# Windowed attention with a squared-ReLU feed-forward on one core: the attention probabilities of nine chunks are transposed by DVE in 32 by 32 blocks

## The chip, the cores and the metric

The kernel runs on one core of one Trainium2 chip. Its time is the device time of one launch in microseconds (us); the median of several runs counts. A core has these engines, each with its own in-order queue: PE (TensorE, matmuls; its weight loads are shown apart as PEld), DVE (VectorE), ACT (ScalarE), POOL (GpSimd) and SP (SyncE, which here issues all DMAs). They wait for each other through semaphores. PSUM is the memory that PE writes; SBUF holds everything else.

## The reference, cut to what matters

```python
B, H, S, D = 4, 8, 768, 64        # batch, heads, positions, head width
block, window = 32, 16            # nb = S // block = 24 blocks
k_sum = k.reshape(B, H, nb, block, D).max(axis=3)
v_sum = v.reshape(B, H, nb, block, D).mean(axis=3)
scores_l = scale * q @ k.T        # kept only where |i - j| < window
scores_s = scale * q @ k_sum.T + log(block)
a = softmax(concatenate([scores_l, scores_s]))
attn = a @ concatenate([v, v_sum])
x = attn.transpose(0, 2, 1, 3).reshape(B * S, H * D)      # 3072 x 512
r = maximum(x @ w_in, 0)                                  # 512 -> 2048
out = (s * r * r + b) @ w_out                             # 2048 -> 512
```

## The kernel before

The 3072 rows are worked off in 12 chunks `c` of T = 256 rows, three to a batch. A chunk has eight heads as four pairs `p`; a pair's two heads `e` lie in the two halves of the 128 partitions. A chunk's rows are four subtiles of 64; each sees a window of 96 keys and the 24 block maxima, so KR = 120 columns.

The attention of one pair goes through these helpers. `scores` (L280) multiplies queries by the 120 keys into PSUM (`ps`). `masked` (L306) lets DVE add the mask and take the extreme of each row, `exps` (L328) is the exponential on ACT, and `normalize` (L336) multiplies by the reciprocal of the sum on DVE. The result `pr` holds 128 rows (two subtiles) in each of four parts of 120 columns. The values matmul needs the 120 columns on the partitions, so `transposes` (L344) turns each part on PE into PSUM (`pt`), and `turned` (L355) copies 120 by 512 from there to SBUF (`pT`) on ACT. `values` (L371) multiplies `pT` by `vw`, the 96 windowed rows of v and below them the 24 block means; a pair takes 16 matmuls of PE, 64 for a chunk. `attended` and `attended_low` make the high and low parts (`xh`, `xl`) of the result on ACT and DVE.

The block means of a batch are made once, in the step before its first chunk's values: `v_sum` (L168) sums blocks on DVE (`vhalf`, six instructions), `v_mean` (L174) scales on ACT (`vmean`) and sends the rows by SP's DMAs to `vsum`, and `fill_v` (L260) copies them into `vw` on POOL. The sums free the buffers for the last loads of v (`load_v`), which stand in SP's queue ahead of the loads of `vw` and `qk` and of the DMAs to `vsum`. `fill_k` copies the maxima into the keys on POOL.

The feed-forward treats the 2048 hidden columns as 16 steps `f` of 128, and two of them as a double block `q` (q0 to q7). `hidden` makes `ph` in PSUM (L434, three matmuls for each of four parts, as high and low parts are multiplied apart), four steps to a hidden block. `activate` is ReLU and square on ACT (L442, L448), `scaled` is s and b on POOL (L455), and `upper_rows` and `lower_rows` make `gh` and `gl` on DVE (L219, L466). `project` (L478) multiplies them by w_out into `po`.

While PE does the feed-forward of chunk c-1, the attention of chunk c is made beside it. The order on all engines is written out: every call is put down with a step (16 to a chunk, `base` is the step before the chunk's first) and a kind, and calls are issued by step and then by kind. For chunks up to c = 2 and the first hidden steps a list by hand (`FIRST_ORDER`) is used. In a chunk's cycle PE does a hidden block (12 x 4 matmuls), a projection (24), and so on, four times; at step `base + 16` stand the values of chunk c and the scores of chunk c+1. The transposes of pairs 0 and 1 stand at step `base + 8`, those of pairs 2 and 3 at `base + 12`, each behind a hidden block.

Of the kernel before, what the change touches and what calls it, by code (L numbers as in the profile page):

```python
# [11 lines left out]
F32 = mybir.dt.float32  # L12
# [7 lines left out]
P = 128  # L20
B, H, S, D = 4, 8, 768, 64
DM, DFF = 512, 2048
BLOCK = 32
WINDOW = 16
SUB = 64
WIN = SUB + 2 * WINDOW
NB = S // BLOCK
KR = WIN + NB
NSUB = 4
T = NSUB * SUB  # L30
# [14 lines left out]
def windowed_attention_then_relu2_ffn(ctx, tc, qk, vwin, kt, vt, kq, vrow, wp, out):  # L45


    nc = tc.nc
# [5 lines left out]
    p2 = ctx.enter_context(tc.tile_pool(name="p2", bufs=2))  # L54
# [29 lines left out]
    def mask_of(st):  # L84
        return mask_first if st == 0 else mask_last if st == NST - 2 else mask_mid
# [3 lines left out]
    def at(step, order, fn, *args):  # L89
        plan[step].append((order, len(plan[step]), fn, args))  # L90
# [5 lines left out]
    for base, sign in ((0, 1), (BLOCK - 1, -1)):  # L96
        nc.gpsimd.affine_select(
            out=mean4[:, NB - 4 : NB], in_=mean4[:, NB - 4 : NB], compare_op=ALU.is_ge, fill=0.0,
            base=base, pattern=[[-sign * BLOCK, 4]], channel_multiplier=sign,
# [117 lines left out]
    def copy(by_dve, out_, in_):  # L217
        if by_dve:
            nc.vector.tensor_copy(out_, in_)  # L219
        else:  # L220
            nc.scalar.copy(out_, in_)  # L221
# [7 lines left out]
    def place(c):  # L229
        return c // PER_B, c % PER_B  # L230

    sb_of = {}
    qk_t, vw_t, ps_of, pr_of, mn_of, sm_of, pt_of, pT_of, o_of, xt, xl = ({} for _ in range(11))
# [42 lines left out]
    def together(c):  # L276

        return c >= 2
# [27 lines left out]
    def masked(c, p, j):  # L306
        _, ci = place(c)
        if j == 0 and c == 0:
            t = stage.tile([P, 4 * KR + 8], F32, name="pr0", tag="stage")
            pr_of[c, p] = t[:, : 4 * KR].rearrange("p (n k) -> p n k", k=KR)  # L310
            mn_of[c, p], sm_of[c, p] = t[:, 4 * KR : 4 * KR + 4], t[:, 4 * KR + 4 :]
        elif j == 0:
            t = p2.tile([P, 4 * KR + 16], F32, name="pr", bufs=4)
            pr_of[c, p] = t[:, : 4 * KR].rearrange("p (n k) -> p n k", k=KR)
            mn_of[c, p] = p2.tile([P, 4], F32, name="mn", bufs=4)
            sm_of[c, p] = p2.tile([P, 4], F32, name="sums", bufs=4)
        for e in range(2):
            n = 2 * e + j
            nc.vector.tensor_tensor_reduce(  # L319
                out=pr_of[c, p][:, n, :], in0=ps_of[c, p][e][:, j, :], in1=mask_of(NSUB * ci + 2 * j),  # L320
                scale=-1.0 / math.sqrt(D), scalar=3.0e38, op0=ALU.add, op1=ALU.min,
                accum_out=mn_of[c, p][:, n : n + 1],
            )
        if j == 1:
            ps_of.pop((c, p))
            qk_t.pop((c, p))
# [9 lines left out]
    def normalize(c, p, other=False):  # L336
# [4 lines left out]
        pr = pr_of[c, p]  # L341
        nc.vector.tensor_tensor(pr, pr, rs.unsqueeze(2).to_broadcast([P, 4, KR]), ALU.mult)  # L342

    def transposes(c, p):  # L344
        pr = pr_of.pop((c, p))
        if c == 2:
            pt_of[c, p] = ps_s.tile([P, 4 * P], F32, name="pt", tag="ps")
        elif together(c) and p % 2:
            pt_of[c, p] = ps_v.tile([P, 4 * P], F32, name="pt", tag="pav")
        else:  # L350
            pt_of[c, p] = ps_t.tile([P, 4 * P], F32, name="pt")
        for n in range(4):
            nc.tensor.transpose(pt_of[c, p][:KR, n * P : (n + 1) * P], pr[:, n, :], ident)  # L353

    def turned(c, p, other=False):  # L355
        if c == 0 and p > 1:
            pT_of[c, p] = held["vn", 1][:KR, 1024 + 512 * (p - 2) : 1024 + 512 * (p - 1)]
        else:
            pT_of[c, p] = p2.tile([KR, 4 * P], F32, name="pT", bufs=4)
        copy(other, pT_of[c, p], pt_of.pop((c, p))[:KR])  # L360

    def values_of_means(p):
        pT, o = pT_of.pop((0, p)), o_of[0, p]
        for i in range(NSUB):
            for e in range(2):
                nc.tensor.matmul(
                    o[64 * e : 64 * e + 64, i * SUB : (i + 1) * SUB], vsum[0][0:KR, 2 * p + e],
                    pT[:, e * T + i * SUB : e * T + (i + 1) * SUB], start=False, stop=(i == NSUB - 1),
                )

    def values(c, p):  # L371
        vw, pT = vw_t.pop((c, p)), pT_of[c, p] if c == 0 else pT_of.pop((c, p))
        if c == 0 and p % 2:
            o_of[c, p] = ps_po.tile([P, DM], F32, name="pav", tag="po")
        elif c < 2 or p % 2 == 0:
            if c == 2:
                o_of[c, p] = ps_s.tile([P, 2 * T], F32, name="pav", tag="ps")
            elif together(c) and p:
                o_of[c, p] = ps_t.tile([P, 2 * T], F32, name="pav", tag="pt")
            else:  # L380
                o_of[c, p] = ps_v.tile([P, 2 * T], F32, name="pav")
            if c > 1:
                o_of[c, p + 1] = o_of[c, p][:, T:]
        o = o_of[c, p]
        for i in range(NSUB):
            for e in range(2):
                oi, pi = o[64 * e : 64 * e + 64, i * SUB : (i + 1) * SUB], pT[:, e * T + i * SUB : e * T + (i + 1) * SUB]
                if c == 0:
                    nc.tensor.matmul(oi, vw[0:WIN, e, i, :], pi[0:WIN], start=(i == 0), stop=False)
                else:  # L390
                    nc.tensor.matmul(oi, vw[:KR, e, i, :], pi, start=True, stop=True)  # L391

    def attended_part(c, p):
        kcs = slice(p, p + (1 if c < 2 else 2))
# [93 lines left out]
        nc.sync.dma_start(out[r0 : r0 + P, :], o)  # L488


    LOAD, SPLIT, ATT, NEXT, WEIGHTS, HID, PE_ATT, CHAIN, VISIT, PROJ, EVICT = range(11)


    FIRST = -100
# [25 lines left out]
    def of(fn, *more):  # L520
# [4 lines left out]
        "i": of(load_weights, "in"), "o": of(load_weights, "out"), "w": of(load_weights, "in", "out"),  # L525
        "u": load_unit, "x": load_values, "L": load_k,
        "W": keep_warm, "K": k_max, "k": fill_k, "Z": scores_of_maxima, "S": scores, "M": masked, "E": exps,
        "N": normalize, "T": transposes, "C": turned, "V": values, "U": values_of_means, "R": mean_of_rows,
        "F": mean_done, "t": fill_v, "X": attended, "y": attended_low, 
        "Ai": of(scale_weights, "in"), "Ao": of(scale_weights, "out"), "A": of(scale_weights, "both"),  # L530
# [20 lines left out]
    def then(step, order, fn, *args):  # L551
        if (fn, args) not in ahead:
            at(step, order, fn, *args)

    for c in range(2, NC):
        bi, ci = place(c)
        for p in range(NPAIR):
            base, v_at = NF * (c - 1) - 1, (9, 10, 4, 5)[p]
            tr = 8 + 4 * (p // 2)
            lags = (1, 1, 1, 2, (12, 13, 11, 11)[p], tr, tr, 16, 17)  # L560
            m, e0, e1, n, fv, tr, tu, va, xa = (base + lag for lag in lags)
            if ci == 0:
                then(base - 12 + p, LOAD, load_k, bi, p)
                then(base - 7 + p, ATT, k_max, bi, p)
                if p < 2:
                    for third in range(3):
                        then(base + v_at - 5 + third, LOAD, load_v, bi, p, third)
                        then(base + v_at - 1 + third // 2, ATT, v_sum, bi, p, third)
                    then(base + v_at + 1, ATT, v_mean, bi, p)
            then(base - 6, LOAD, load_unit, c, p)  # L570
            then(base + v_at, LOAD, load_values, c, p)
            then(base - 2, ATT, fill_k, c, p)
            for j in range(2):
                then(base, VISIT, scores, c, p, j)
                then(m, NEXT if p < 2 else ATT, masked, c, p, j)
                then((e0, e1)[j], NEXT if p < 2 else ATT, exps, c, p, j)
            then(n, ATT, normalize, c, p)
            then(fv, ATT, fill_v, c, p)
            then(tr, PE_ATT, transposes, c, p)
            then(tu, CHAIN, turned, c, p)  # L580
            then(va, VISIT, values, c, p)
            if p % 2 == 0:
                then(xa, ATT, attended, c, p)
                then(xa, ATT, attended_low, c, p)
# [3 lines left out]
    for i in range(NF, NC * NF):  # L588
        c, f = divmod(i, NF)
# [69 lines left out]
```

## Time and profile before

| | |
|---|---|
| median of 3 runs | 624.66 us (624.11 to 624.74) |
| the profiled execution | 624.84 us |
| its span, first to last instruction | 622.7 us |
| distance between two chunks' values on PE (from 313.77 to 363.41 us) | 49.64 us |

The profile describes one execution. Its page gives the busy time of each engine, the granted TensorE clock in 40 slices, the chain of work that ended last, and groups of like instructions with count, busy time and mean duration. A timeline lists single instructions: start in us, length in us, engine, line, output and inputs, and in brackets how long the engine had been idle and what released it. The length includes the filling and emptying of an engine's pipeline, so on PE and DVE an instruction may start before the one ahead has ended; the distance of starts tells the rate.

### The profile page before, as it was taken

Reading aid. Unit: us, or ns where it says so; the run is one execution under the profiler, and the core shown is the slowest. Engines: PE = TensorE matmul, PEld = TensorE weight load, DVE = VectorE, ACT = ScalarE, POOL = GpSimd, SP = SyncE. Lnnn points to the kernel's source line nnn. Section 1 sums busy time; section 2 is a strip of 40 time slices with the busy share of each in tenths; the row PEclk is TensorE's granted clock in tenths of the full one; section 3 lists DMA queues with packets and bytes.
Section 4 is the critical chain, followed back from the end, with each engine's and each line's share of the span. In section 5 each row is a group of like instructions: output and inputs, shape, how many; then the busy total and the mean of one; then the engine's idle time right before and its main releaser. Section 6 shows DMA issues by size and latency. Waiting matters only on the chain.

```text
span 622.7 us, 13558 instructions
## 1 busy us (share of the span) xinstructions
PE 612.3 (98%) x5384; PEld 553.7 (89%) x5384; DVE 292.2 (47%) x838; ACT 294.2 (47%) x748; POOL 135.5 (22%) x257
## 2 busy tenths in 40 slices
PE   6999999999999999999999999999999999999997
PEld 5788999899999989998999899999998998899896
DVE  6999988755441262363262243444426126212211
ACT  5999997353353352363264253334335336222221
POOL 4320013111411410411311401321141041131110
PEclk9999999999999999999999999999999999999999
DMA  8998722126005107005304012500700500200000
GB/s 343 379 402 343 274 79 99 46 79 214 20 15 168 31 14 275 2 18 146 124 19 150 33 45 91 187 18 35 233 20 2 182 1 19 85 2 1 35 2 34
DMA packets 26991, 66.41 MB, mean 107 GB/s; under 512 B 3824, under 2 KB 3824, under 8 KB 26928
## 3 DMA queue, kind: packets, MB, share of 16 engines
q1 hardware_dynamic: 26928, 65.54, 30.1%
q8 instruction: 42, 0.69, 0.5%
q14 instruction: 21, 0.17, 0.1%
HBM read 59.09 MB, written 6.29 MB: 105 GB/s over the span
## 4 chain that ended last, share of the span: by engine, by line
PE 93%; ACT 3%; DMA 2%; DVE 1%; issue 0%; SPq 0%; DVEq 0%; ACTq 0%
PE po L478 43%; PE ph L434 41%; PE pav L391 3%; PE pt L353 3%; PE ps L301 3%; ACT pr L332 1%; DMA wraw<-in_wp_dram 1%; DMA kq<-in_kq_dram 1%; DVE pr L342 0%; ACT wraw L122 0%; ACT wraw L123 0%; DVE ksum L156 0%; ACT vsum L221 0%; ACT r L442 0%; ACT r L453 0%
## 5 line engine op out<-in xcount | busy, mean ns | idle before, releaser
L219 DVE CAST gh<-r 128x512 fp32r<-128x512 f32 x88 | 37.7, 428 | 278.0 <-POOL r L455 269.1
L455 POOL TENSOR_SCALAR r<-r,sb_col 128x512 f32<-128x512 f32 x85 | 67.9, 799 | 408.2 <-ACT r L448 308.9
L478 PE MATMUL po<-wh,gl 128*128 128x512 f32 x384 | 153.3, 399 | 0.0
L478 PE MATMUL po<-wh,gh 128*128 128x512 f32 x384 | 151.2, 394 | 0.0
L478 PE MATMUL po<-wl,gh 128*128 128x512 f32 x384 | 150.2, 391 | 0.0
L442 ACT ACTIVATE r<-ph 128x512 f32<-128x512 f32 x93 | 55.8, 600 | 191.4 <-PE ph L434 178.7
L434 PE MATMUL ph<-xh,wl 128*128 128x256 f32 x760 | 118.8, 279 | 0.2 <-ACT r L442 0.2
L434 PE MATMUL ph<-xl,wh 128*128 128x256 f32 x760 | 117.5, 277 | 0.0
L434 PE MATMUL ph<-xh,wh 128*128 128x256 f32 x760 | 117.4, 277 | 0.0
L434 PEld LDWEIGHTS ph<-xh,wl 128*128 128x128 f32 x760 | 104.6, 188 | 5.6 <-ACT r L442 0.7
L434 PEld LDWEIGHTS ph<-xl,wh 128*128 128x128 f32 x760 | 101.0, 188 | 0.0
L434 PEld LDWEIGHTS ph<-xh,wh 128*128 128x128 f32 x760 | 100.4, 188 | 0.0
L478 PEld LDWEIGHTS po<-wh,gh 128*128 128x128 f32 x384 | 72.2, 188 | 15.5
L478 PEld LDWEIGHTS po<-wh,gl 128*128 128x128 f32 x384 | 72.2, 188 | 14.8 <-issue 1.4
L478 PEld LDWEIGHTS po<-wl,gh 128*128 128x128 f32 x384 | 72.2, 188 | 14.0
L332 ACT ACTIVATE pr<-pr,mn 128x120 f32<-128x120 f32 x176 | 66.9, 382 | 19.4 <-DVE mn L319 19.3
L466 DVE TENSOR_TENSOR gl<-r,gh 128x512 fp32r<-128x512 f32 x96 | 67.9, 708 | 4.1 <-ACT gh L221 1.3
L448 ACT ACTIVATE r<-r 128x512 f32<-128x512 f32 x92 | 58.2, 632 | 5.7 <-DVE r L444 2.9
L263 POOL COPY vw<-vsum 24x256 f32<-24x256 f32 x88 | 47.3, 572 | 29.6 <-DMA vsum<-vmean 10.2
L221 ACT COPY pT<-pt 120x512 f32<-120x512 f32 x44 | 23.9, 585 | 30.0 <-PE pt L353 29.8
L221 ACT COPY o<-po 128x512 f32<-128x512 f32 x23 | 13.5, 585 | 46.1 <-PE po L478 45.0
L342 DVE TENSOR_TENSOR pr<-pr,rs 128x480 f32<-128x480 f32 x48 | 32.1, 669 | 2.4 <-ACT pr L332 0.5
(86 smaller groups left out, 505.2 us busy)
## 6 DMA issues: line engine op xcount, KB each, us to landing
wraw<-in_wp_dram SPq DMA_DIRECT2D x32, 512.0 KB
qk<-in_qk_dram SPq DMA_DIRECT2D x44, 369.0 KB
vw<-in_vwin_dram SPq DMA_DIRECT2D x48, 256.0 KB
out_dram<-o SPq DMA_DIRECT2D x24, 256.0 KB
kraw<-in_kt_dram SPq DMA_DIRECT2D x12, 384.0 KB
vraw<-in_vt_dram SPq DMA_DIRECT2D x12, 252.0 KB
kq<-in_kq_dram SPq DMA_DIRECT2D x4, 512.0 KB
vraw<-in_vt_dram SPq DMA_DIRECT2D x6, 264.0 KB
```

Of the source, the lines that this page charges most:

```text
L219: nc.vector.tensor_copy(out_, in_)
L221: nc.scalar.copy(out_, in_)
L263: nc.gpsimd.tensor_copy(vw_t[c, p][WIN:KR, e], vsum[bi][WIN : WIN + NB, 2 * p + e, :].unsqueeze(1).to_broadcast([NB, NSUB, D]),)
L301: nc.tensor.matmul(o, qi, kw[r, i, :], start=True, stop=True)
L332: nc.scalar.activation(pr, pr, AF.Exp, bias=mn_of[c, p][:, n : n + 1], scale=-1.0, accum_out=sm_of[c, p][:, n : n + 1])
L342: nc.vector.tensor_tensor(pr, pr, rs.unsqueeze(2).to_broadcast([P, 4, KR]), ALU.mult)
L434: nc.tensor.matmul(ph, w[:, kc * P : (kc + 1) * P], x[:, kc], start=(n == 0), stop=(n == len(terms) - 1))
L442: nc.scalar.activation(r, ph, AF.Relu)
L448: nc.scalar.activation(r, r, AF.Square)
L455: (nc.vector if other else nc.gpsimd).tensor_scalar(g, g, s_col, b_col, ALU.mult, ALU.add)
L466: nc.vector.tensor_tensor(gl, g, gh.bitcast(F32), ALU.subtract)
L478: nc.tensor.matmul(po[c, t], a[:, t * P : (t + 1) * P], w[:, 512:], start=(f == 0 and n == 0), stop=(f == NF - 1 and n == len(terms) - 1),)
```

## The change

For chunks c > 2 the eight transposes on PE and the copy by ACT go. In their place `turned_blocks` issues, for each pair and each group `a` of 32 rows, four `nc.vector.transpose`: each takes 32 partitions and 32 columns of all four parts, turns the four 32 by 32 blocks, and writes them to the partitions 32k to 32k + 31 of `pT`. 120 columns are not a multiple of 32, so the fourth takes columns 96 to 127 through a view shifted by 8; eight columns behind the last part are set to zero by POOL (`memset`), and rows 120 to 127 of `pT` are not read. A new kind of call, TURN, stands behind CHAIN and ahead of VISIT; the sixteen calls of a chunk are spread over the steps `base + 3` to `base + 15`. `pT` has 128 partitions in place of 120.

```diff
             pr_of[c, p] = t[:, : 4 * KR].rearrange("p (n k) -> p n k", k=KR)
+            if turns_on_dve(c):
+                nc.gpsimd.memset(t[:, 4 * KR : 4 * KR + 8], 0.0)
+                wide_of[c, p] = t[:, 8 : 4 * KR + 8].rearrange("p (n k) -> p n k", k=KR)
...
+    def turns_on_dve(c):
+        return c > 2
+
+    def turned_blocks(c, p, a):
+
+        if a == 0:
+            pT_of[c, p] = p2.tile([P, 4 * P], F32, name="pT", bufs=4)
+        to = pT_of[c, p].rearrange("p (n q) -> p n q", q=P)
+        rows = slice(BLOCK * a, BLOCK * (a + 1))
+        for k in range(4):
+            src = (pr_of[c, p][rows, :, BLOCK * k : BLOCK * (k + 1)] if k < 3 else wide_of[c, p][rows, :, KR - BLOCK :])
+            nc.vector.transpose(to[BLOCK * k : BLOCK * (k + 1), :, rows], src)
...
-            pT_of[c, p] = p2.tile([KR, 4 * P], F32, name="pT", bufs=4)
-        copy(other, pT_of[c, p], pt_of.pop((c, p))[:KR])
+            pT_of[c, p] = p2.tile([P, 4 * P], F32, name="pT", bufs=4)
+        copy(other, pT_of[c, p][:KR], pt_of.pop((c, p))[:KR])
...
-                    nc.tensor.matmul(oi, vw[:KR, e, i, :], pi, start=True, stop=True)
+                    nc.tensor.matmul(oi, vw[:KR, e, i, :], pi[:KR], start=True, stop=True)
...
-    LOAD, SPLIT, ATT, NEXT, WEIGHTS, HID, PE_ATT, CHAIN, VISIT, PROJ, EVICT = range(11)
+    LOAD, SPLIT, ATT, NEXT, WEIGHTS, HID, PE_ATT, CHAIN, TURN, VISIT, PROJ, EVICT = range(12)
...
-            then(tr, PE_ATT, transposes, c, p)
-            then(tu, CHAIN, turned, c, p)
+            if turns_on_dve(c):
+                for a in range(4):
+                    then(base + 3 + (4 * p + a) * 13 // 16, TURN, turned_blocks, c, p, a)
+            else:
+                then(tr, PE_ATT, transposes, c, p)
+                then(tu, CHAIN, turned, c, p)
```

Where this moves instructions is seen at three places. The first is PE, between a hidden block and the projection behind it, in the middle of a chunk (c = 7). A row is the line, the operation, output and inputs, and the shape; "x4" are four alike. Before:

```order
L434 MATMUL ph<-xh,wl 128x256 x4
L434 MATMUL ph<-xl,wh 128x256 x4
L434 MATMUL ph<-xh,wh 128x256 x4
L353 MATMUL pt<-ident,pr 120x128 x8
L478 MATMUL po<-wh,gl 128x512
L478 MATMUL po<-wl,gh 128x512
L478 MATMUL po<-wh,gh 128x512
```

Now:

```order
L455 MATMUL ph<-xh,wl 128x256 x4
L455 MATMUL ph<-xl,wh 128x256 x4
L455 MATMUL ph<-xh,wh 128x256 x4
L499 MATMUL po<-wh,gl 128x512
L499 MATMUL po<-wl,gh 128x512
L499 MATMUL po<-wh,gh 128x512
```

The eight transposes of two pairs are gone from PE, and nothing stands in their place.

The second place is DVE in a chunk that begins a batch (c = 9), from `gh` and `gl` of q2 on, through the sums of v, to `gh` of q4. Before:

```order
L219 CAST gh<-r 128x512
L466 TENSOR_TENSOR gl<-r,gh 128x512
L172 TENSOR_REDUCE vhalf<-vraw 96x22
L172 TENSOR_REDUCE vhalf<-vraw 96x21
L219 CAST gh<-r 128x512
L466 TENSOR_TENSOR gl<-r,gh 128x512
L172 TENSOR_REDUCE vhalf<-vraw 96x21
L172 TENSOR_REDUCE vhalf<-vraw 96x22
L172 TENSOR_REDUCE vhalf<-vraw 96x21 x2
L219 CAST gh<-r 128x512
```

Now, from the twelve transposes that stand behind `gl` of q2 on:

```order
L360 STREAM_TRANSPOSE pT<-pr 32x4x32 x12
L172 TENSOR_REDUCE vhalf<-vraw 96x22
L172 TENSOR_REDUCE vhalf<-vraw 96x21
L219 CAST gh<-r 128x512
L487 TENSOR_TENSOR gl<-r,gh 128x512
L360 STREAM_TRANSPOSE pT<-pr 32x4x32 x4
L172 TENSOR_REDUCE vhalf<-vraw 96x21
L172 TENSOR_REDUCE vhalf<-vraw 96x22
L172 TENSOR_REDUCE vhalf<-vraw 96x21
L360 STREAM_TRANSPOSE pT<-pr 32x4x32 x4
L172 TENSOR_REDUCE vhalf<-vraw 96x21
L219 CAST gh<-r 128x512
```

Transposes now stand ahead of the first sum and between the sums.

The third place is DVE at the end of every chunk, from `gh` of q6 to `xl` of the finished chunk. Before:

```order
L219 CAST gh<-r 128x512
L466 TENSOR_TENSOR gl<-r,gh 128x512
L219 CAST gh<-r 128x512
L466 TENSOR_TENSOR gl<-r,gh 128x512
L407 TENSOR_TENSOR xl<-pav,xh 128x512 x2
```

Now, with the eight transposes that stand behind `gl` of q5 as the first row:

```order
L360 STREAM_TRANSPOSE pT<-pr 32x4x32 x8
L219 CAST gh<-r 128x512
L487 TENSOR_TENSOR gl<-r,gh 128x512
L360 STREAM_TRANSPOSE pT<-pr 32x4x32 x8
L219 CAST gh<-r 128x512
L487 TENSOR_TENSOR gl<-r,gh 128x512
L428 TENSOR_TENSOR xl<-pav,xh 128x512 x2
```

The last eight transposes of pair 3 stand between `gl` of q6 and `gh` of q7.

More of the change, by code (lines that the diff above doesn't have):

```diff
@@ L342, in normalize @@
         nc.vector.tensor_tensor(pr, pr, rs.unsqueeze(2).to_broadcast([P, 4, KR]), ALU.mult)
+    wide_of = {}
+    def turns_on_dve(c):
[8 more added lines that the diff above has]
+            nc.vector.transpose(to[BLOCK * k : BLOCK * (k + 1), :, rows], src)
+        if a == 3:
+            pr_of.pop((c, p))
+            wide_of.pop((c, p))
     def transposes(c, p):
@@ L367, in values_of_means @@
                     o[64 * e : 64 * e + 64, i * SUB : (i + 1) * SUB], vsum[0][0:KR, 2 * p + e],
-                    pT[:, e * T + i * SUB : e * T + (i + 1) * SUB], start=False, stop=(i == NSUB - 1),
+                    pT[:KR, e * T + i * SUB : e * T + (i + 1) * SUB], start=False, stop=(i == NSUB - 1),
                 )
```

## The prediction

> **What bounds the kernel now.** I read the busy line of the page first, then the chain that ended last, then the timeline of PE around the parts that the diff touches.
>
> ```profile
> PE 612.3 (98%) x5384; PEld 553.7 (89%) x5384; DVE 292.2 (47%) x838; ACT 294.2 (47%) x748; POOL 135.5 (22%) x257
> ...
> PE 93%; ACT 3%; DMA 2%; DVE 1%; issue 0%; SPq 0%; DVEq 0%; ACTq 0%
> PE po L478 43%; PE ph L434 41%; PE pav L391 3%; PE pt L353 3%; PE ps L301 3%; ACT pr L332 1%; DMA wraw<-in_wp_dram 1%; DMA kq<-in_kq_dram 1%; DVE pr L342 0%; ACT wraw L122 0%; ACT wraw L123 0%; DVE ksum L156 0%; ACT vsum L221 0%; ACT r L442 0%; ACT r L453 0%
> ```
>
> PE is the bound, and the transposes (pt) are 3% of its chain. Whatever leaves PE is gained, unless PE then waits for what replaces it. So there are two questions: what the transposes cost on PE, and when DVE delivers.
>
> **What leaves PE.** The timeline of PE, first where a hidden block meets a projection without transposes between, then with eight:
>
> ```profile
> 328.65 0.39 PE L478 MATMUL po<-wh,gl 128*128 128x512 f32 x1
> 328.88 0.39 PE L478 MATMUL po<-wl,gh 128*128 128x512 f32 x1
> ...
> 339.62 1.04 PE L353 MATMUL pt<-ident,pr 128*120 128x128 f32 x8
> 340.41 0.48 PE L478 MATMUL po<-wh,gl 128*128 128x512 f32 x1
> 340.73 0.40 PE L478 MATMUL po<-wl,gh 128*128 128x512 f32 x1
> ```
>
> Eight transposes hold PE from 339.62 to 340.41, 0.79 us, and the first projection matmul behind them takes 0.32 in place of 0.23: 0.88 us. Two such groups in each of nine chunks (c = 3 to 11) make 18 x 0.88 = **15.8 us** off PE, 1.76 per chunk. The copies from PSUM leave ACT too; ACT is not the bound and I count them at nothing.
>
> **What one block transpose costs.** DVE gets 16 instructions per pair, 64 per chunk, each 32 partitions by 4 x 32 columns. No row of before is one; the nearest DVE rows (groups, then two masks in the timeline, as start and length):
>
> ```profile
> L340 DVE RECIPROCAL rs<-rs 128x4 f32<-128x4 f32 x48 | 8.5, 176 | 1.3
> ...
> L342 DVE TENSOR_TENSOR pr<-pr,rs 128x480 f32<-128x480 f32 x48 | 32.1, 669 | 2.4 <-ACT pr L332 0.5
> ...
> L319 DVE DVE_READ_ACCUMULATOR2_ANT mn<- 128x1 f32 x176 | 14.7, 83 | 0.0
> ...
> 318.35 0.27 DVE L319 CUSTOM_DVE_ANT_0 pr<-ps,mask_mid 128x120 f32<-128x120 f32 x1
> ...
> 318.55 0.28 DVE L319 CUSTOM_DVE_ANT_0 pr<-ps,mask_mid 128x120 f32<-128x120 f32 x1
> ```
>
> 4 columns take 176 ns and 480 take 669: 1.04 ns a column on a base of 172. So 128 columns last about 0.30 us. Back to back, independent masks of 120 columns follow each 0.20 us, so overlap could bring 0.21; without its accumulator read of 0.08 a mask would be 0.12, the lower end. With a gap of 0.04 after each, 0.34 is the upper end. I take **0.30**, no overlap: each block writes to another partition group than the one before, which no row here does, so I do not count on the masks' overlap. [...]
>
> In total, DVE has room:
>
> ```profile
> 312.70:362.30 49.60, 49.60 (x435) 45.27 (x434) 17.40 (x62) 20.21 (x56) 11.51 (x21) 1.00 0.19 64
> ...
> 411.90:461.60 49.70, 49.70 (x435) 45.38 (x434) 21.94 (x68) 20.72 (x58) 11.03 (x21) 1.00 0.30 90
> ```
>
> The columns are PE, PEld, DVE, ACT, POOL: 64 x 0.30 = 19.2 us on top of 17.40 or 21.94 fit into the 49.6 - 1.76 = 47.8 of a chunk. But DVE is in order, and order decides.
>
> **The wait in a plain chunk.** Block transposes stand between the pairs of gh and gl that DVE makes from the hidden rows. The last eight of pair 3 stand behind gh and gl of the seventh double block (q6), and the values matmuls of pair 3 need them:
>
> ```profile
> 357.86 0.63 PE L434 MATMUL ph<-xh,wl 128*128 128x256 f32 x4
> ...
> 363.41 2.08 PE L391 MATMUL pav<-pT,vw 120*64 120x64 f32 x64
> 365.42 1.87 PE L301 MATMUL ps<-qk 64*64 64x120 f32 x64
> ...
> 360.84 0.60 ACT L442 ACTIVATE r<-ph 128x512 f32<-128x512 f32 x1 [6.50 <-PE ph L434]
> ...
> 363.01 0.43 DVE L219 CAST gh<-r 128x512 fp32r<-128x512 f32 x1 [6.47 <-POOL r L455]
> 363.47 0.69 DVE L466 TENSOR_TENSOR gl<-r,gh 128x512 fp32r<-128x512 f32 x1
> ```
>
> Count from the start of the last hidden block, 357.86. q6 is its first half; through ACT and POOL gh starts at +5.15 and gl ends at +6.30. Eight transposes bring +8.70, the signal 0.05 more. PE starts the values at +5.55 and spends 2.01 us on 64, so it stands before the third matmul of pair 3, the 51st, at +7.12. It waits 8.75 - 7.12 = **1.63 us**. Six chunks are of this kind (c = 4, 5, 7, 8, 10, 11): 9.8 us. The k-maxima in c = 5 and 8 lie in DVE's pause before q6.
>
> **The wait in a chunk that begins a batch** (c = 3, 6, 9). There DVE also sums the blocks of v, and a chain through SP and POOL hangs on it. c = 6 in before:
>
> ```profile
> 290.82 1.63 DVE L172 TENSOR_REDUCE vhalf<-vraw 96x22 f32<-96x704 f32 x2
> ...
> 291.73 0.31 SPq L165 DMA_DIRECT2D vraw<-in_vt_dram  x1
> ...
> 293.85 2.28 SPq L245 DMA_DIRECT2D qk<-in_qk_dram  x4
> ...
> 303.50 0.26 ACT L178 ACTIVATE vmean<-vhalf 96x64 f32<-96x64 f32 x1 [2.86 <-DMA vsum<-vmean]
> ...
> 307.97 1.09 POOL L263 COPY vw<-vsum 24x256 f32<-24x256 f32 x3 [0.31 <-DMA vsum<-vmean]
> 309.16 0.77 POOL L455 TENSOR_SCALAR r<-r,sb_col 128x512 f32<-128x512 f32 x1
> ...
> 309.97 0.43 DVE L219 CAST gh<-r 128x512 fp32r<-128x512 f32 x1 [7.21 <-POOL r L455]
> ...
> 312.57 0.77 POOL L455 TENSOR_SCALAR r<-r,sb_col 128x512 f32<-128x512 f32 x1 [0.16 <-ACT r L448]
> ...
> 313.77 2.08 PE L391 MATMUL pav<-pT,vw 120*64 120x64 f32 x64
> ```
>
> SP issues the next load of v (291.73) when the first sum frees its buffer; behind it in SP's queue stand the loads of qk and then the means (vsum), whose landing lets ACT make the second mean, whose landing lets POOL fill vw, and only then POOL scales q5 (309.16). Now twelve transposes stand ahead of the first sum, so this chain comes 12 x 0.30 = 3.6 us later. From POOL's start on q5: gh starts 0.81 later, gh and gl 1.15, eight transposes 2.4, gh and gl of q6 1.15, eight more 2.4, signal 0.05: 7.96. PE would stand at the 51st matmul 1.57 after a start that is 1.76 earlier: 0.19 before its old start. So the wait is 3.6 + 7.96 + 0.19 = 11.75 less the distance from POOL's q5 to the values in before. That is 4.61 for c = 6; for c = 3 and 9:
>
> ```profile
> 160.35 0.77 POOL L455 TENSOR_SCALAR r<-r,sb_col 128x512 f32<-128x512 f32 x1
> ...
> 164.89 2.08 PE L391 MATMUL pav<-pT,vw 120*64 120x64 f32 x64
> ...
> 456.64 0.77 POOL L455 TENSOR_SCALAR r<-r,sb_col 128x512 f32<-128x512 f32 x1
> ...
> 462.67 2.09 PE L391 MATMUL pav<-pT,vw 120*64 120x64 f32 x64
> ```
>
> 4.54 and 6.03: waits of 7.14, 7.21 and 5.72, together 20.1 us. The waits for POOL's filled vw at pairs 0 and 1 end earlier and are inside them.
>
> **Behind the wait** nothing more comes:
>
> ```profile
> 317.15 1.28 DVE L407 TENSOR_TENSOR xl<-pav,xh 128x512 fp32r<-128x512 f32 x2
> ...
> 323.19 0.64 PE L434 MATMUL ph<-xh,wl 128*128 128x256 f32 x4
> ```
>
> From the start of the values to the next hidden block are 9.42 us, 7.85 from the 51st matmul. DVE has gh and gl 1.15, xl 1.28 and 16 masks at 0.20 = 3.2 to do before that block: 5.6. POOL's memsets of the eight columns lie in its idle time (22% busy), and gh's own wait on POOL covers them for the transposes.
>
> **The sum:** -15.8 + 9.8 + 20.1 = +14.1 us. The profiled execution took 624.84 (span 622.7), 0.2 above the median of 624.66: **638.9 us**. With 0.34 a block the waits are 6 x 1.95 and 23.4: 644.1. No difference is what lies within 0.2%, about what a measurement of this kernel can tell.
>
> **The rivals.**
> *Overlap:* blocks follow each 0.21, as masks do. Plain waits 0.91; in the others the chain comes 2.52 later, and POOL's q6, 3.41 behind q5 (309.16 to 312.57) and 0.80 long with its signal, now ends last: 2.52 + 3.41 + 0.80 + 1.15 + 1.68 + 0.05 + 0.19 = 9.8 less the distances, 14.2 in all. 19.7 against 15.8: 628.7. For: the masks' rows. Against: the partition groups.
> *Short blocks, faster:* one mechanism, the price of a block on DVE. At the lower end of 0.12 the plain wait is 0.19, and the others, by the sum just given with 1.44 and 0.96 for 2.52 and 1.68, are 8.8 together: 9.9 against 15.8, so 618.9. The sign turns where a block costs 0.17 or less. For: a mask without its accumulator read. Against: base and slope above; even 4 columns take 176 ns alone.
> *Cooling:* PE's pauses of 6 to 7 us slow what follows. At the start of before, after 4.1 us without work:
>
> ```profile
> 4.14 0.92 PE L304 MATMUL ps<-kq 64*64 64x96 f32 x16 [4.14 <-DMA kq<-in_kq_dram]
> ...
> 10.72 0.56 PE L304 MATMUL ps<-kq 64*64 64x96 f32 x16
> ...
> PEclk9999999999999999999999999999999999999999
> ```
>
> Sixteen matmuls of the same shape take 0.92 and later 0.56, although the page's row of the granted clock shows no dip. If some 6 us after each long wait run so, each loses 6 x (1 - 0.56/0.92) = 2.3 us, three lose 7: 646. [...]
> *Slow blocks:* a transpose takes two passes a column, 0.43. Plain waits 2.67, the others 31.0, and DVE's 27.5 on 21.94 no longer fit: 656 or more.
>
> **How the numbers follow.** Chances: forecast 0.35, cooling 0.22, overlap 0.18 (a third of it drifting to no difference, as its 3.9 us is the thinnest margin), short blocks 0.17, slow blocks 0.08. Faster 0.17, same 0.06, slower 0.77. The range runs from 620, which leaves out about half of the short blocks, to 652, which leaves out the slow blocks and the worst of cooling.
>
> **What would show it.** Right: pt gone from PE for c > 2; a block near 0.30, start to start; PE waiting for DVE's transposes before the 51st values matmul, 1.6 us in six chunks and 6 to 7 in three; the sums of v 3.6 us later. Wrong: blocks at 0.17 or less, or no longer waits in c = 3, 6, 9 because the loads land early all the same.

## The result, and the profile after

The changed kernel took **651.45 us** (median of four runs, 648.66 to 652.49), the kernel before 624.7 beside it: a ratio of **1.042** [1.038, 1.046], some 27 us slower. The profiled execution took 652.49 us with a span of 650.8, against 624.84 and 622.7. One execution of a later experiment (the second version of the matmuls in the pauses) took 880.92 us at a mean granted clock of 0.658, and is left out of that experiment's median.

The page of the changed kernel, the lines that answer to those of before: busy time of each engine, the slices of PE and of the granted clock, the engines of the chain that ended last, and two groups.

```profile
PE 611.1 (94%) x5240; PEld 548.6 (84%) x5240; DVE 466.1 (72%) x1414; ACT 276.1 (42%) x712; POOL 132.6 (20%) x293
...
PE   6999999999699999999879999999969999998997
...
PEclk9999999999799999999979999999977999999999
...
PE 17%; issue 4%; DVE 4%; DMA 2%; POOL 1%; ACT 0%; SPq 0%; POOLq 0%; ACTq 0%
...
L360 DVE STREAM_TRANSPOSE pT<-pr 32x128 f32<-32x128 f32 x576 | 174.1, 302 | 8.1
...
L412 PE MATMUL pav<-pT,vw 120*64 120x64 f32 x704 | 30.9, 237 | 29.6 <-DVE pT L360 22.3
```

576 block transposes of 302 ns have come to DVE, and PE is idle for 29.6 us ahead of values matmuls. PE has 144 instructions less (5240 against 5384) but only 1.2 us less of busy time, and the clock row dips in four slices, at the places where the row of PE dips. In before it was all 9s. The chain's shares add up to 28% because it could be followed back only to about the last third of the span.

The waits of PE, with the time in total, how often, and the longest:

```profile
PE pav L412 <- DVE pT L360: 22.3, 12, 3.5
PE pav L412 <- POOL vw L263: 7.1, 8, 2.6
```

In before the values waited for neither. These 29.4 us stand in the values of the nine chunks. PE's timeline in a plain chunk (c = 4) and in one that begins a batch (c = 6) shows the two kinds:

```profile
219.07 1.74 PE L412 MATMUL pav<-pT,vw 120*64 120x64 f32 x52
222.42 0.57 PE L412 MATMUL pav<-pT,vw 120*64 120x64 f32 x12 [1.61 <-DVE pT L360]
222.92 1.87 PE L301 MATMUL ps<-qk 64*64 64x120 f32 x64
...
319.89 1.02 PE L412 MATMUL pav<-pT,vw 120*64 120x64 f32 x16 [0.53 <-POOL vw L263]
321.82 0.33 PE L412 MATMUL pav<-pT,vw 120*64 120x64 f32 x2 [0.91 <-POOL vw L263]
322.63 1.15 PE L412 MATMUL pav<-pT,vw 120*64 120x64 f32 x30 [0.48 <-POOL vw L263]
324.80 0.48 PE L412 MATMUL pav<-pT,vw 120*64 120x64 f32 x4 [1.02 <-DVE pT L360]
328.74 0.91 PE L412 MATMUL pav<-pT,vw 120*64 120x64 f32 x12 [3.46 <-DVE pT L360]
329.58 3.48 PE L301 MATMUL ps<-qk 64*64 64x120 f32 x64
```

In c = 4 one wait of 1.61 us stands in the values, in pair 3, and the scores behind it last what they lasted before (1.87). In c = 6 five waits add up to 6.40 us, and the scores behind them last 3.48: the same 64 matmuls, nearly twice as long. The windows view there (stretch, then busy time of PE, PEld, DVE, ACT and POOL, then the granted clock):

```profile
322.00:326.00 4.00, 1.78 (x36) 1.31 (x35) 3.84 (x11) 1.70 (x3) 3.08 (x10) 0.82 0.17 65
326.00:330.00 4.00, 1.26 (x20) 1.14 (x24) 3.83 (x12) 0.30 (x1) 0.10 (x1) 0.50 0.00 0
330.00:334.00 4.00, 4.00 (x66) 3.52 (x59) 1.98 (x11) 0.86 (x4) 0.00 (x0) 0.50 0.02 4
334.00:336.00 2.00, 2.00 (x9) 1.61 (x8) 2.00 (x21) 2.00 (x12) 0.00 (x0) 0.80 0.00 0
```

In stretches of 1 us in c = 3 the clock reads 1.00 or 0.50, and between them where it changes (0.77 from 167 to 168 us). From the means of the four rows the clock was half for 1.44 + 4 + 4 + 0.80 = 10.24 us: it fell inside the pause and came back some 6 us after PE was busy again. Read the same way, the half-clock stretch lasts 6.8 us in c = 3 and 13.7 us in c = 9.

Where the time went, from the distances of the starts of PE's blocks, all from the values of c = 2 to the end of PE's work (us, after minus before):

```text
                                                    forecast   measured
transposes and the projection starts behind them      -15.8      -15.8
values of the six plain chunks                         +9.8      +11.0
values of c = 3, 6, 9, with POOL waits ahead          +20.1      +25.9
scores and projections behind c = 3, 6, 9               0         +5.8
hidden blocks, POOL waits taken off                     0         +1.5
sum                                                   +14.1      +28.4
```

The measured sum fits the spans, 650.8 - 622.7 = 28.1, as the stretch begins 0.2 us earlier after the change.

The chain that ended last, in order of time, for c = 9 of the changed kernel (start, length, what); it is the chain that the prediction wrote down, here by way of the load of `vw`:

```profile
460.21 0.30 DVE pT L360
460.54 1.64 DVE vhalf L172 x2
...
463.05 5.53 DMA vw<-in_vwin_dram
468.60 5.04 DMA vsum<-vmean
...
475.52 3.81 DMA vsum<-vmean
...
479.80 1.09 POOL vw L263 x3
480.99 0.78 POOL r L476
...
489.09 0.32 DVE pT L360
489.45 0.91 PE pav L412 x12
```

Block transposes delay the sum of v; the landings of a load of `vw` and of two groups of means follow (14.4 us together), then POOL's fills and q5, then `gh`, `gl` and sixteen transposes, and PE's values end it.

### The profile page after: what moved, and what is told of

Same layout as the page of the kernel before. It is cut to its first block, busy times and chain, and to the rows that moved or that the text cites. A ratio compares the mean times of both kernels' runs of the same rounds, so it can differ in the third digit from the quotient of the medians.

```text
span 650.8 us, 13845 instructions
## 1 busy us (share of the span) xinstructions
PE 611.1 (94%) x5240; PEld 548.6 (84%) x5240; DVE 466.1 (72%) x1414; ACT 276.1 (42%) x712; POOL 132.6 (20%) x293
## 5 line engine op out<-in xcount | busy, mean ns | idle before, releaser
L360 DVE STREAM_TRANSPOSE pT<-pr 32x128 f32<-32x128 f32 x576 | 174.1, 302 | 8.1
L499 PEld LDWEIGHTS po<-wl,gh 128*128 128x128 f32 x384 | 72.6, 189 | 14.1
L412 PE MATMUL pav<-pT,vw 120*64 120x64 f32 x704 | 30.9, 237 | 29.6 <-DVE pT L360 22.3
L412 PEld LDWEIGHTS pav<-pT,vw 120*64 120x64 f32 x704 | 25.8, 146 | 34.9 <-DVE pT L360 24.2
L263 POOL COPY vw<-vsum 24x256 f32<-24x256 f32 x88 | 41.8, 509 | 44.2 <-DMA vsum<-vmean 28.1
```

The source lines that it names most:

```text
L263: nc.gpsimd.tensor_copy(vw_t[c, p][WIN:KR, e], vsum[bi][WIN : WIN + NB, 2 * p + e, :].unsqueeze(1).to_broadcast([NB, NSUB, D]),)
L360: nc.vector.transpose(to[BLOCK * k : BLOCK * (k + 1), :, rows], src)
L412: nc.tensor.matmul(oi, vw[:KR, e, i, :], pi[:KR], start=True, stop=True)
L499: nc.tensor.matmul(po[c, t], a[:, t * P : (t + 1) * P], w[:, 512:], start=(f == 0 and n == 0), stop=(f == NF - 1 and n == len(terms) - 1),)
```

## The experiments

Each is an edit of the changed kernel. The kernel before took 624.57 us in the first set of runs and 625.16 in the second; the ratios are against it.

**Block transposes in the six plain chunks alone.** PE's transposes stay in c = 3, 6, 9.

```diff
-        return c > 2
+        return c > 2 and c % 3 != 0
```

> Block transposes only in the six chunks that do not begin a batch (c = 4, 5, 7, 8, 10, 11); the other three keep the transposes on PE. Theory, order on DVE: per chunk 1.76 us leave PE and the pause before the last values of pair 3 costs 1.84 (start to start in the changed kernel), so 6 x 0.08 = +0.5 us: 625.2, no difference. No stretch of half clock, as no pause is longer than 2 us. Rival, the load of DVE as such (the 27 us of the changed kernel spread evenly over its nine chunks): 6/9 of it, 643.

Measured 625.99 us, ratio 1.0023 [1.0014, 1.0032]. PE's wait in this run:

```profile
PE pav L412 <- DVE pT L360: 9.8, 6, 1.7
```

Six waits of 1.6 us, as forecast. The values take 3.85 us in place of 2.01 there, 1.84 more, so a wait costs 0.2 above its idle time; twelve groups of transposes bring 10.55. In the profiled execution the granted clock stayed at 1.00 until PE's work had ended. The plain chunks alone are within 0.3% of even (0.8 us above the 625.2 expected), and the loss must come from the other three.

**Block transposes in c = 3, 6, 9 alone.**

```diff
-        return c > 2
+        return c > 2 and c % 3 == 0
```

> Block transposes only in the three chunks that begin a batch (c = 3, 6, 9). Theory, order on DVE plus cooling: -5.3 us of transposes, +26 us of values blocks that last longer, +6 us of slow matmuls behind them at half clock: about 651, and three stretches of half clock. Order on DVE without cooling: 645. Rival, the load of DVE as such: 3/9 of 27 us, 634.

Measured 647.65 us, ratio 1.037 [1.036, 1.039]: three chunks cost 23 us, with six groups of transposes saved (5.3). The clock's row in this run:

```profile
PEclk9999999999699999999969999999988999999999
```

Three dips, one behind each pause; the scores behind them take 3.41 us each from start to start in place of 1.80. So the cooling that was expected is there. The time is below the 651 expected with it, as the values of the three chunks, POOL waits included, last 23.5 us longer in place of 26. Both parts together (1.4 and 23.1) make 24.5 of the whole change's 26.8, so they act on each other little.

**All transposes called early:** none at steps 6 to 8, where the first sums of v stand, and none in the last four steps of a chunk.

```diff
-                    then(base + 3 + (4 * p + a) * 13 // 16, TURN, turned_blocks, c, p, a)
+                    then(base + (3, 3, 4, 4, 5, 5, 5, 9, 9, 9, 9, 11, 11, 11, 11, 11)[4 * p + a], TURN, turned_blocks, c, p, a)
```

> The same 576 block transposes in all nine chunks, issued at other steps: the sixteen calls of a chunk at base + 3, 3, 4, 4, 5, 5, 5, 9, 9, 9, 9, 11, 11, 11, 11, 11, so none stands behind gh of q5 or q6 and none between gl of q2 and the first sum of v. Theory, order: DVE does the same work (some 466 us busy), no pause of PE is left, and the whole 15.8 us show: 609, clock 1.00 throughout. Rival, load or contention of the transposes with other engines: it stays near 651, or at 630 and more.

Measured **610.06 us**, ratio 0.977 [0.975, 0.978], faster than before. Its busy line, the group of transposes, and the only waits of its values (L412):

```profile
PE 597.6 (98%) x5240; PEld 539.3 (89%) x5240; DVE 466.6 (77%) x1414; ACT 276.5 (45%) x712; POOL 135.6 (22%) x293
...
L360 DVE STREAM_TRANSPOSE pT<-pr 32x128 f32<-32x128 f32 x576 | 174.3, 303 | 8.8
...
PE pav L412 <- POOL vw L263: 1.2, 2, 0.7
```

DVE does the same 174 us of transposes at the same 303 ns, and PE waits for none of them. So neither the price of a block nor DVE's load made the kernel slower: the place in DVE's order did. The values take 2.02 us in every chunk from c = 4 on, and 3.77 in c = 3.

**Matmuls in the pauses, to keep the clock up.** Products of the identity, whose results nothing reads, stand ahead of the values of pairs 0, 1 and 3 in c = 3, 6, 9: work added, in a first version far too much, in a second about half (10, 5, 0 and 15 in place of the four counts below).

```diff
     def values(c, p):
...
+        if c > 2 and c % 3 == 0 and p != 2:
+            w = ps_s.tile([P, 4 * P], F32, name="warm", tag="ps")
+            for _ in range((20, 10, 0, 34)[p]):
+                nc.tensor.matmul(w[:, :P], ident, ident, start=True, stop=True)
```

> [...] Theory, cooling: no or hardly any stretch of half clock, and the 6 to 8 us of slow matmuls go: about 644. Rival, the pauses alone: no gain, 651 or a little more.

Measured 666.8 us, ratio 1.067 [1.066, 1.069]: a miss. Each such product stands in the trace as two matmuls of 0.11 us, 0.23 for both (twenty take 4.55 us from start to start in c = 3), so 128 such rows made 14.8 us in each of three chunks and overfilled the pause. The clock stayed at 1.00, but this time settles nothing on what the half clock cost.

> As e4_warm with 10, 5 and 15 extra matmuls ahead of the values of pairs 0, 1 and 3 in c = 3, 6, 9: they took 0.456 us each there (two passes of 0.228), so they fill 13.7 / 3 x 3 = 13.7 us a chunk at most if I count wrongly again, and 30 x 0.228 = 6.8 if 0.228 is one of them; the pause is 7.4 to 10. Theory, cooling: no stretch of half clock; from values to scores 9.6 us as before, but scores back at 1.80 in place of 2.83 to 3.41 and the first projection at 5.61 in place of up to 6.43: 5 to 6 us less than the changed kernel, 645 to 646. Rival, the pauses alone: 651 or more.

Measured 644.32 us (median of three executions), ratio 1.031 [1.029, 1.034]. Its PE in c = 6:

```profile
317.79 2.39 PE L409 MATMUL warm<-ident 128*128 128x128 f32 x20
...
326.67 0.34 PE L416 MATMUL pav<-pT,vw 120*64 120x64 f32 x4
327.73 0.57 PE L416 MATMUL pav<-pT,vw 120*64 120x64 f32 x12 [0.72 <-DVE pT L360]
328.23 1.87 PE L301 MATMUL ps<-qk 64*64 64x120 f32 x64
```

From the end of the hidden block to the scores are 328.23 - 317.79 = 10.44 us, against 329.58 - (319.89 - 0.53) = 10.22 without the added work, so the pause covers it. A product takes 0.23 to 0.24 us, not the 0.456 of the expectation: the thirty of c = 6 take 7.2. The scores take 1.87 again, the clock is 1.00 throughout, and nothing else in the order has moved. So the half clock comes from PE's lack of work in the pause. What it costs: the two profiled executions differ by 8.2 us (652.49 and 644.32); 5.8 of it is the scores and projections behind the pauses, and 2.8 is c = 9, where the chain through the DMAs ended earlier this time; c = 3 and 6 lost 0.3 of it again.

**The sums of v first.** The four calls of pair 1 move from steps 6 to 8 to step 9, behind the first sums; all others stay, the late ones of pair 3 too.

```diff
-                    then(base + 3 + (4 * p + a) * 13 // 16, TURN, turned_blocks, c, p, a)
+                    then(base + (3, 3, 4, 5, 9, 9, 9, 9, 9, 10, 11, 11, 12, 13, 14, 15)[4 * p + a], TURN, turned_blocks, c, p, a)
```

> The changed kernel with the calls 4, 5 and 6 of a chunk (the twelve block transposes behind gl of q2) moved to step base + 9, behind the first sums of v; the last eight stay behind gl of q6. Theory, the chain from the first sum of v over SP, DMA and POOL to q5: in c = 3, 6, 9 the pauses shrink by 3.6 us or more, to 2 to 4, too short for half clock, and the plain chunks keep 1.84: 11 + 10 - 15.8 = +5, 630. Rival, the pause comes only from what stands behind q5 and q6 on DVE: nothing changes, 651.

Measured 644.55 us, ratio 1.031 [1.028, 1.034], between the two expectations. The values with the POOL waits ahead of them shrank in c = 3, 6 and 9 by 1.5, 4.3 and 5.4 us, so the sums' place does carry a part of the wait. But the waits that are left (4.8, 3.7 and 4.1 us) were not too short for half clock, as had been expected: the scores behind them take 3.02, 2.74 and 3.41 us from start to start. That the waits didn't shrink more shows in DVE in c = 6:

```profile
297.92 1.64 DVE L172 TENSOR_REDUCE vhalf<-vraw 96x22 f32<-96x704 f32 x2
...
303.06 6.34 DVE L360 STREAM_TRANSPOSE pT<-pr 32x128 f32<-32x128 f32 x20
309.43 0.85 DVE L172 TENSOR_REDUCE vhalf<-vraw 96x21 f32<-96x672 f32 x1
```

The first sums are early, but twenty transposes now stand ahead of the last sum, and the second mean waits for that. And a new loss came: in c = 5 and 8, where DVE also makes the maxima of the keys, the plain wait grew to 2.24 and 2.58 us, and the clock halved behind both. In all it fell five times in this run, three times in the changed kernel. PE's timeline and the windows in c = 5:

```profile
270.87 0.57 PE L412 MATMUL pav<-pT,vw 120*64 120x64 f32 x12 [2.24 <-DVE pT L360]
271.37 3.24 PE L301 MATMUL ps<-qk 64*64 64x120 f32 x64
```

```profile
268.27:271.68 3.41, 1.17 (x37) 0.96 (x36) 3.23 (x11) 0.71 (x3) 1.00 (x5) 1.00 0.26 79
271.68:275.09 3.41, 3.41 (x65) 3.04 (x54) 1.98 (x8) 0.53 (x2) 0.00 (x0) 0.50 0.00 0
```

A pause of 2.24 us was enough, where the plain waits of 1.50 to 1.70 us in all these runs never were.

**Two pairs in turn.** As in the early version, but the transposes of two pairs alternate block by block, so that every second one reads and writes the same groups of 32 partitions as the one ahead of it.

```diff
         for k in range(4):
-            src = (pr_of[c, p][rows, :, BLOCK * k : BLOCK * (k + 1)] if k < 3 else wide_of[c, p][rows, :, KR - BLOCK :])
-            nc.vector.transpose(to[BLOCK * k : BLOCK * (k + 1), :, rows], src)
+            for pp in (p, p + 1):
...
+                nc.vector.transpose(to[BLOCK * k : BLOCK * (k + 1), :, rows], pr[rows, :, cols])
...
-                for a in range(4):
-                    then(base + 3 + (4 * p + a) * 13 // 16, TURN, turned_blocks, c, p, a)
+                for a in range(4 if p % 2 == 0 else 0):
+                    then(base + (3, 5, 5, 9, 11, 11, 11, 11)[2 * p + a], TURN, turned_blocks, c, p, a)
```

> As e3_early, but the block transposes of two pairs are interleaved: the same 32 rows and the same 32 columns of both, one behind the other, so every second one reads and writes the partition group of the one ahead; steps base + 3, 5, 5, 9, 11, 11, 11, 11 for the eight calls of 8. Theory, an instruction is held only where the partition group changes: distances of starts alternate between about 0.21 and 0.32, and DVE is some 27 us less busy. Rival, every block transpose costs 0.317: DVE is as busy as in e3_early. The time is 608 to 610 by both, since PE does not wait there; without the pause of 1.75 us that c = 3 has left in e3_early it is 608.

Measured **608.62 us**, ratio 0.974 [0.972, 0.975], the fastest of all. Its busy line, the group of transposes, and eight of them in DVE's timeline:

```profile
PE 597.6 (98%) x5240; PEld 538.9 (89%) x5240; DVE 435.1 (72%) x1414; ACT 276.1 (45%) x712; POOL 136.2 (22%) x293
...
L362 DVE STREAM_TRANSPOSE pT<-pr 32x128 f32<-32x128 f32 x576 | 142.9, 281 | 4.0
...
336.95 2.04 DVE L362 STREAM_TRANSPOSE pT<-pr 32x128 f32<-32x128 f32 x8
```

DVE saves 31 us, 27 were expected. Eight take 2.04 where eight of the change's order take 2.52: with the last one's own length taken off, 0.25 and 0.32 from start to start on average. The starts do alternate, but by 0.24 and 0.27 (means of the single records) in place of the 0.21 and 0.32 expected: the second of two on the same groups starts 0.07 before the first has ended, and lasts 0.26 itself; the one that changes the groups starts 0.01 after the end of the one ahead. The time gains little by it (1 to 2 us), as PE already waited for almost nothing in the early version.

## Why the prediction was right, and where it fell short

**The time** lies in the range, with luck: 651.45 is 0.55 us below the upper end of 652, and one of the four executions (652.49) was above it. The sum of +14.1 us is about half of the +26.8 measured. Two of its steps failed, both told below: the distance in c = 3, 6, 9 taken as fixed, and nothing put down for what runs behind the wait; the range reached so far up to hold most of the cooling rival, at 646.

**What leaves PE** was right: 18 groups of 0.88 us are 15.8, and the blocks show 15.8. **The price of a block**, taken as 0.30, is 302 ns, and no overlap is what the trace shows: 0.316 from start to start, where every block changes its partition group and starts 0.01 us after the one ahead has ended. With pairs in turn only every second block changes it and starts so late; the others start 0.07 before the one ahead has ended. The two rivals that rested on cheaper blocks, and the one with two passes, fell with that row.

**The plain waits** were right: 1.63 forecast, 1.50 to 1.69 in the six chunks, in pair 3, before the 53rd matmul in place of the 51st. Their price was 11.0 rather than 9.8, because each cost 0.2 more than its idle time.

**The waits in c = 3, 6, 9** had the right mechanism and the wrong size, above all in c = 9. The chain view shows the links that were named, with the load of `vw` as the one ahead of the means, and the experiment on the sums moved the waits in the direction named. The twelve transposes ahead of the first sum hold it for 3.8 us (forecast 3.6), in DVE's timeline of the changed kernel:

```profile
297.58 3.77 DVE L360 STREAM_TRANSPOSE pT<-pr 32x128 f32<-32x128 f32 x12
301.38 1.64 DVE L172 TENSOR_REDUCE vhalf<-vraw 96x22 f32<-96x704 f32 x2
```

As added time of the values, POOL waits included, they are 7.4, 8.2 and 10.3 us in c = 3, 6 and 9 against 7.21, 7.14 and 5.72. The step that failed is the use of before's distance from the sums to q5 as fixed. From the first sum to POOL's q5 in c = 9, before:

```profile
439.70 1.63 DVE L172 TENSOR_REDUCE vhalf<-vraw 96x22 f32<-96x704 f32 x2
...
450.98 0.26 ACT L178 ACTIVATE vmean<-vhalf 96x64 f32<-96x64 f32 x1 [1.44 <-DVE gh L219]
```

and after:

```profile
460.54 1.64 DVE L172 TENSOR_REDUCE vhalf<-vraw 96x22 f32<-96x704 f32 x2
...
473.71 0.26 ACT L178 ACTIVATE vmean<-vhalf 96x64 f32<-96x64 f32 x1 [6.85 <-DMA vsum<-vmean]
...
480.99 0.77 POOL L476 TENSOR_SCALAR r<-r,sb_col 128x512 f32<-128x512 f32 x1
```

Before, 456.64 - 439.70 = 16.94 us; after, 20.45. The second mean came 1.9 us later behind the first sum, and q5 1.6 later behind the mean; after the change both wait for the landing of the means' DMAs. In c = 3 and 6 the same distance went from 18.53 to 17.49 and from 18.34 to 18.90. These three shifts (-1.0, +0.6, +3.5) make 3.0 of the 5.8 us by which the waits exceed their forecast. For the rest there is an estimate alone: 28 blocks at 0.316 in place of 0.30 are 0.45 us a chunk, and the last twelve values matmuls, behind the wait and at half clock (0.91 where a plain chunk has 0.57), some 0.5. The row of before for c = 9 showed the shortest of three such chains, and the prediction took it as it stood. Why these landings vary wasn't tried.

**"Behind the wait nothing more comes"** was wrong. Nothing comes late from DVE, as was argued, but the clock halves, and the scores and projections behind the three pauses lose 5.8 us where the sum had 0. That is the cooling rival: its size (2.3 us a pause) was near the 1.9 measured. It was set aside because no row of before shows it in mid-kernel, but before had no pause there that could show it. The sum of forecast and cooling, 646, is still some 6 short: most of that is c = 9, with 4.6, and the rest the 0.2 beside each wait and the slower hidden blocks, less what cooling was taken too high.

**The sign** was right, and so was what would decide it: the wait that takes the place of the work removed. The change as an idea isn't slow: the same instructions in another order of calls give 610 us.

## What to carry to other kernels

Work that moves from a busy in-order engine to one with room must be placed as well as fit: look up what stands behind it in the new queue, and put it ahead of nothing that a load or another engine waits for. The chain of small DMAs between engines had no fixed length here (16.94 to 20.45 us from the first sum to q5), so a forecast through one takes at least the longest seen, not the row at hand. A pause of PE is priced with what runs behind it (5.8 us behind the three pauses). Here the same instructions called at other places turned a loss of 4% into a gain of 2.3%.

## What the hardware showed that was not expected

**The clock fell while PE still had some work.** In the 3.41 us ahead of its fall (the length of the shortest half-clock stretch, in c = 5 of the experiment on the sums) PE was still busy for 1.5 us in c = 6 (first row), and for 2.0 us in c = 3 of the experiment with block transposes in c = 3, 6, 9 alone (second row). In c = 4 of the changed kernel, around a plain wait, it was busy for 1.8 us, and the clock held (third row):

```profile
321.15:324.56 3.41, 1.47 (x32) 1.20 (x32) 3.28 (x10) 1.70 (x3) 3.35 (x8) 1.00 0.20 77
...
162.12:165.53 3.41, 2.01 (x44) 1.60 (x46) 2.24 (x6) 0.94 (x2) 3.18 (x8) 1.00 0.20 77
...
219.00:222.41 3.41, 1.81 (x54) 1.60 (x52) 3.23 (x11) 1.70 (x3) 0.89 (x4) 1.00 0.44 140
```

The other falls of the changed kernel followed 1.60 us (c = 3) and 0.94 (c = 9), those of the experiment on the sums 0.00 to 1.26. In the plain chunks the clock held at as little as 1.72 (c = 11 of the experiment on them). So busy time by itself gives no limit: the clock fell behind 2.01 us and held behind 1.72. What decides the fall stays open, as no run took it apart.

The half-clock stretches (6.8, 10.24, 13.7 us, and 3.41 in c = 5 of the experiment on the sums) are near 2, 3, 4 and 1 times 3.41 us. In that experiment the falls, at 169.28, 271.68, 326.29, 428.69 and 479.89 us, lie 30, 16, 30 and 15 times 3.413 us apart, which is a third of the 10.24 us. In the changed kernel the three falls, at 167.53, 324.54 and 481.56 us, lie 157.01 us apart, 46 times 3.413. What sets this length was not shown.

**A slower hidden block at full clock.** In some chunks every hidden block takes 5.65 us in place of 5.46 from start to start, at a granted clock of 1.00. In the changed kernel these are the blocks behind the values of c = 5 and of c = 7, whose own waits are plain ones; the kernel before has two such blocks ahead of the values of c = 3, the changed kernel one. It makes the 1.5 us of the table above. What starts it stays open.
